# Two square-ReLU/leaky layers behind sparse attention: in-place sums, a moved group of products and full-row last values

## The chip, the cores and the metric

One core of one Trainium2 chip runs the whole program. The metric is device microseconds (us) from the first to the last instruction and what lies around them; lower is better. The kernel before takes 1148.19 us, the median of three runs (1145.18 to 1148.43).

## The reference

Attention over 4 batches of 8 heads, 576 positions, head width 64, in which scores more than `tau` below a row's maximum are dropped; then two layers of 512 to 2048 to 512 over the 2304 tokens. All is float32.

```python
scores = scale * np.matmul(q, k.transpose(0, 1, 3, 2))
thresh = np.max(scores, axis=-1, keepdims=True) - tau
scores = np.where(scores >= thresh, scores, -1000000000.0)
attn = softmax(scores)                      # written out in full in the reference
x = (attn @ v).transpose(0, 2, 1, 3).reshape(B * S, H * D)
h = x @ w_in;   x = (s * np.maximum(h, 0.0) ** 2 + b) @ w_out           # first layer
h = x @ w_in2;  g = np.maximum(h, 0.0) + alpha * np.minimum(h, 0.0)     # second layer
return g @ w_out2
```

## The kernel before, in words

**Who sets the order.** Nothing is scheduled while the chip runs. `add` records each step as a task with its engine, an assumed duration, the buffers that it reads and writes and a rank; a task may have two ways (DVE or POOL, say). `Plan.run` (L142) plays the tasks through once, when the program is built: whenever an engine is free, it takes the ready task of lowest rank whose buffers can be had. The order that comes out stands in each engine's queue, and an engine works its queue strictly in that order: an instruction that waits holds up all behind it. `SOON` is the lowest of the usual ranks, `LATER` a large one. A pool of buffers is a `Slots`; `caps` says how many of them a group may hold ("x": inputs of the second layer, "g": its hidden values).

**Stages, by the time in the trace.** Attention of batch 0 (pairs of heads 0 to 3) runs in plain fp32 up to about 145 us, the other batches in split form up to about 480 us, with the first part of layer 1 between them; the rest of layer 1 runs to 770 us (`blocks_b`, six blocks of 384 tokens); the first product of layer 2 to 958 us (three pairs of blocks); its second product to 1141.6 us (nine sub-blocks of 2 x 128 tokens).

**Split products.** Outside the plain attention, each product is three fp32r matmuls: `mm3` (L462) multiplies a low part by a high one, a high by a low, and a high by a high (L463, L464, L465). An operand's high part is an ACT copy to fp32r (L441), its low part the difference, on DVE or POOL (L442).

**Layer 2 by seven products.** Each product of 2 x 2 blocks is made of 7 products of sums of quarters instead of 8 (the Winograd form of Strassen's scheme). `seven` (L417) makes the operands: four sums of quarters (L433; t1 to t4 of inputs, s1 to s4 of hidden values), and for each of seven operands the high and the low part. They are used in the order `TURNS = (1, 2, 5, 6, 3, 7, 4)`; operands 1, 2 and 3 of the inputs are plain quarters, 5, 6, 7 and 4 are t1, t2, t3 and t4. t2 needs t1, and t4 needs t2. Each sum takes a new buffer of group "x" or "g". The quarters are loaded by the SP queue, and a pair's loads wait for the sums of the pair before (`xc`).

**First product of layer 2.** For each pair of blocks and each of eight groups of rows u, PE runs products 1, 2, 5, 6, 3 of this group and products 7 and 4 of the group before (`late7`, `late4`, L1122 and L1131), so that the DVE addition ahead of 7 and 4 (`plus`, L1114) has time. Behind it come the copies out of PSUM (`copy`, L1110) and `leaky` (L1075 to L1077: two ACT, one DVE), whose result goes to memory. The last group has no group behind it: its 7 and 4 follow directly (L1149). Layer 1's last block adds a part kept from earlier to each result (L1036) and stores it.

**Second product.** For each sub-block 4 turns l of 7 products from the hidden values; `copy` and `plus` (L1204) put the seven results together, `both` (L1208, DVE or POOL) adds two buffers, `store` (L1215) sends the rows out on the SP queue.

**Values of batch 0.** For a group of score tiles, `group` (L804) transposes five chunks of the weights (L818, L822), copies each to a buffer (gf or sh, L827) and multiplies it with the chunk's values (`product`, L831). The fifth chunk has only TL = 64 of 128 rows, and its product runs over these:

```python
nc.tensor.matmul(
    o.t[:, :n], lhsT=vt.t[:rows, c].rearrange("p h d -> p (h d)"), rhs=f.t[:rows, :n],
    start=c == 0, stop=c == NK - 1)
```

There are 16 such products (4 pairs, 4 groups each), 8 over 256 columns and 8 over 320. The trace shows each fp32 product as two matmuls.

## Time and profile before

| | |
|---|---|
| runs | 1148.19 us median, 1145.18 to 1148.43 |
| profiled execution | 1149.12 us, of which the span is 1147.1 us |
| PE busy | 1108.4 us, 97% of the span |
| DVE / ACT / POOL busy | 81% / 67% / 31% |
| chain that ended last | PE 66%, DVE 16%, ACT 9%, DMA 4% |
| issue of stores of the result | 56, all on the SP queue |

PE is the engine to watch: the chain of work that ended last is two thirds PE. A busy PE is not a PE at its peak, since the end of a matmul is modelled and matmuls overlap. What counts is the distance from one start to the next. In a stretch without waits it is 0.17 us for a split matmul of 384 columns and 0.12 us for one of 256. Times in a view are microseconds from the start of the span; "idle before" in brackets names what the engine waited for.

### The profile page before, as it was taken

How to read it: one execution, taken by the hardware profiler on the slowest of the kernel's cores; microseconds unless marked ns; L12 is line 12 of the kernel's file. 1: busy time of each engine (PE TensorE's matmuls, PEld its weight loads, DVE VectorE, ACT ScalarE, POOL GpSimd, SP SyncE). 2: the span in 40 equal slices, each digit the busy share in tenths (PEclk: the TensorE clock that was granted, in tenths of full speed). 3: DMA queues.
4: the chain of work that ended last, by engine and by line, in shares of the span. 5: the costliest groups of instructions: out<-in, count | busy, mean ns of one | idle time of the engine just before them, and what ended most of it. 6: DMA issues, size and time to landing. Idle time of an engine off the chain costs nothing.

```text
span 1147.1 us, 22073 instructions
## 1 busy us (share of the span) xinstructions
PE 1108.4 (97%) x7536; PEld 1052.3 (92%) x7536; DVE 934.2 (81%) x2040; ACT 764.2 (67%) x1744; POOL 358.7 (31%) x477
## 2 busy tenths in 40 slices
PE   8989999999999999999999999999999999999998
PEld 6667799999989999999999999999999998999998
DVE  5798887888978889847877788488975989899882
ACT  4787886877777878744444476366877987556551
POOL 2356663654664735500000012020211332112111
PEclk9999999999999999999999999998999999999999
DMA  5643354446435343134466564346724455455541
GB/s 120 162 141 122 102 142 110 110 100 156 101 88 129 100 109 93 37 109 155 123 218 210 182 214 157 124 133 206 261 103 162 138 189 161 116 143 153 139 116 37
DMA packets 183921, 156.92 MB, mean 137 GB/s; under 512 B 72192, under 2 KB 160768, under 8 KB 183808
## 3 DMA queue, kind: packets, MB, share of 16 engines
q1 hardware_dynamic: 183808, 155.51, 47.3%
q8 instruction: 59, 0.97, 0.4%
q14 instruction: 54, 0.44, 0.1%
HBM read 91.24 MB, written 44.56 MB: 118 GB/s over the span
## 4 chain that ended last, share of the span: by engine, by line
PE 66%; DVE 16%; ACT 9%; DMA 4%; issue 3%; SPq 1%; POOL 0%; POOLq 0%; DVEq 0%; ACTq 0%
PE bank L463 9%; PE bank L464 9%; PE bank L465 9%; PE bank_b L465 7%; PE bank_b L464 7%; PE bank_b L463 7%; PE sc L714 5%; PE bank L818 4%; PE bank L865 3%; DVE e L730 3%; DVE mx L724 2%; PE bank L831 2%; ACT e L728 2%; PE bank L822 1%; DVE wa L442 1%
## 5 line engine op out<-in xcount | busy, mean ns | idle before, releaser
L730 DVE SCALAR_TENSOR_TENSOR e<-sc,mx,e 128x576 f32<-128x576 f32 x144 | 116.6, 814 | 21.7 <-ACT e L728 18.5
L818 PE MATMUL bank<-eyes,e 128*128 128x128 f32 (+1 forms) x640 | 121.7, 277 | 1.7 <-DVE e L730 0.9
L728 ACT ACTIVATE e<-sc,mx 128x576 f32<-128x576 f32 x144 | 105.6, 737 | 26.4 <-DVE mx L724 25.4
L724 DVE TENSOR_REDUCE mx<-sc 128x1 f32<-128x576 f32 x144 | 107.4, 751 | 11.5 <-PE sc L714 10.2
L846 POOL TENSOR_TENSOR gl<-gf,gh 128x256 fp32r<-128x256 f32 (+1 forms) x96 | 78.0, 816 | 60.7 <-ACT gh L844 29.3
L818 PEld LDWEIGHTS bank<-eyes,e 128*128 128x128 f32 (+1 forms) x640 | 75.8, 134 | 21.9 <-issue 6.3
L463 PE MATMUL bank<-gt,wa 128*128 128x256 f32 (+1 forms) x271 | 84.9, 313 | 1.6 <-ACT rest L501 0.9
L463 PE MATMUL bank<-xt,wa 128*128 128x256 f32 (+1 forms) x266 | 82.8, 311 | 2.5 <-ACT rest L501 1.3
L464 PE MATMUL bank<-gt,wa 128*128 128x256 f32 (+1 forms) x271 | 81.2, 300 | 1.8 <-DVE gt L442 1.6
L465 PE MATMUL bank<-gt,wa 128*128 128x256 f32 (+1 forms) x271 | 80.7, 298 | 0.0
L465 PE MATMUL bank<-xt,wa 128*128 128x256 f32 (+1 forms) x266 | 76.8, 289 | 0.0
L464 PE MATMUL bank<-xt,wa 128*128 128x256 f32 (+1 forms) x266 | 76.7, 288 | 0.0
L726 POOL TENSOR_SCALAR mx<-mx,tau_s 128x1 f32<-128x1 f32 x144 | 46.7, 325 | 82.8 <-DVE mx L724 79.0
L714 PE MATMUL sc<-k,q 128*128 128x288 f32 x272 | 66.3, 369 | 3.4 <-DVE e L730 2.8
L865 PE MATMUL bank<-gl,vt 128*128 128x256 f32 (+1 forms) x192 | 64.4, 336 | 1.2 <-DVE gl L851 0.6
L464 PE MATMUL bank_b<-gt,wa 128*128 128x384 f32 (+1 forms) x169 | 55.3, 327 | 1.6 <-DVE gt L514 1.6
L865 PE MATMUL bank<-gh,vt 128*128 128x256 f32 (+1 forms) x192 | 56.5, 295 | 0.0
L521 ACT ACTIVATE rest<-bank 128x384 f32<-128x384 f32 x39 | 19.1, 490 | 55.6 <-PE bank L465 55.6
L463 PE MATMUL bank_b<-gt,wa 128*128 128x384 f32 (+1 forms) x169 | 55.4, 328 | 0.0
L714 PEld LDWEIGHTS sc<-k,q 128*128 128x128 f32 x272 | 44.2, 193 | 12.2 <-DVE e L730 5.1
L465 PE MATMUL bank_b<-gt,wa 128*128 128x384 f32 (+1 forms) x169 | 55.1, 326 | 0.0
L524 ACT ACTIVATE gt<-rest,b_b,s_b 128x384 fp32r<-128x384 f32 x56 | 39.4, 706 | 23.6 <-DVE rest L522 22.9
(654 smaller groups left out, 4170.5 us busy)
## 6 DMA issues: line engine op xcount, KB each, us to landing
stg<-in_moe_w_in_dram SPq DMA_DIRECT2D x32, 512.0 KB, 3.9
stg<-in_moe_w_out_dram SPq DMA_DIRECT2D x32, 512.0 KB, 3.8
qo<-hq SPq DMA_DIRECT2D x32, 256.0 KB, 4.3
rest<-gf SPq DMA_DIRECT2D x38, 128.0 KB, 3.0
ko<-hk SPq DMA_DIRECT2D x32, 144.0 KB, 2.5
xr<-xs SPq DMA_DIRECT2D x6, 768.0 KB, 4.9
yf<-yb SPq DMA_DIRECT2D x24, 192.0 KB, 3.1
gf<-rest SPq DMA_DIRECT2D x24, 192.0 KB, 1.9
```

The lines of the kernel that those rows point to most:

```text
L463: nc.tensor.matmul(o, lhsT=wl, rhs=mh, start=first, stop=False, skip_group_check=on_top)
L464: nc.tensor.matmul(o, lhsT=wh, rhs=ml, start=False, stop=False, skip_group_check=on_top)
L465: nc.tensor.matmul(o, lhsT=wh, rhs=mh, start=False, stop=last, skip_group_check=on_top)
L524: t = add("ACT", act(n, 2, True), lambda: nc.scalar.activation(g.t[:, 0, :n], r.t[:, :n], AF.Identity, bias=b_b, scale=s_b), (r,), (g,), r ...
L714: nc.tensor.matmul(sp.t[:, x, :HS], lhsT=o[0][:, c], rhs=o[1][:, x * HS:(x + 1) * HS], start=n == 0, stop=n == len(passes) - 1)
L724: add("DVE", dve(S), lambda sp=sp, mx=mx: nc.vector.tensor_reduce(mx.t[:, 0:1], sp.t[:, :, :HS], op=ALU.max, axis=AX.XY, negate=True), (sp ...
L726: t2 = add("POOL", 0.26, lambda mx=mx: nc.gpsimd.tensor_scalar(mx.t[:, 1:2], mx.t[:, 0:1], -1.0, tau_s, op0=ALU.mult, op1=ALU.subtract), ( ...
L728: add("ACT", act(S, 1), lambda sp=sp, mx=mx, e=e: nc.scalar.activation(halves(e.t), sp.t[:, :, :HS], AF.Exp, bias=mx.t[:, 0:1]), (sp, mx), ...
L730: add("DVE", dve(S) + 0.065, lambda sp=sp, mx=mx, e=e, col=col, sums=sums: nc.vector.scalar_tensor_tensor(halves(e.t), sp.t[:, :, :HS], mx ...
L818: nc.tensor.transpose(gt.t[:rows, m:m + P], es[i].t[:, c * P:c * P + rows], ident)
L846: add("POOL", pool2(n), lambda hi=hi, lo=lo, f=f: nc.gpsimd.tensor_tensor(lo.t[:, :n], f.t[:, :n], f32(hi.t[:, :n]), op=ALU.subtract), (f, ...
L865: nc.tensor.matmul(o.t[:, :n], lhsT=w, rhs=m.t[:, :n], start=c == 0 and x == 0, stop=c == NK - 1)
```

## The change

Five things change, in six places of the code.

1. In the first pair of the second layer, the sums take the place of quarters and sums that are no longer needed (t1 over quarter 11, t2 over t1, t3 over quarter 12, t4 over t2); a sum waits for those that read what it overwrites. In all pairs the sums of the inputs run on DVE alone. The caps of "x" and "g" go from 10 to 13 and from 8 to 12.
2. The additions of layer 1's last block get a later rank than before.
3. The last group's product 4 goes behind the first two products of the next stage, in front of its third.
4. `both` runs on DVE alone; a store may be issued by ACT where SP is busy, at rank LATER. As built, 24 of the 56 stores are on ACT.
5. The product of the fifth chunk runs over all 128 rows. The values behind row 64 are set to zero (4 memsets on POOL in place of 4 loads), and the gf and sh buffers are cleared once at the start (4 memsets).

```diff
-    t_s, sm_s = Slots(caps={"x": 10, "g": 8, "q": 6}), Slots()
+    t_s, sm_s = Slots(caps={"x": 13, "g": 12, "q": 6}), Slots()
...
-    def seven(quarters, left, n, tmp, group, to, to_group, rank, later=0.0):
-        have, sums, at = dict(quarters), [], 0.0
-        def ways(r):
-            return [("DVE", dve(n), r), ("POOL", pool2(n), r + later)]
+    def seven(quarters, left, n, tmp, group, to, to_group, rank, engines=("DVE", "POOL"), over={}):
+        have, sums, at, readers = dict(quarters), [], 0.0, {}
+        def ways(es):
+            return [(e, dve(n) if e == "DVE" else pool2(n), rank + at) for e in es]
...
-                b = Buf(tmp, group)
-                def a():
-                    return b.t[:, :n]
-                sums.append(add(ways(rank + at), 0, lambda e: on(e).tensor_tensor(a(), ax(), ay(), op=op), (bx, by), (b,), port=True))
+                if name in over:
+                    b, a = have[over[name]]
+                    after = readers.get(over[name], ())
+                else:
+                    b, after = Buf(tmp, group), ()
+                    def a():
+                        return b.t[:, :n]
+                t = add(ways(engines), 0, lambda e="DVE": on(e).tensor_tensor(a(), ax(), ay(), op=op), (bx, by), (b,), after=after, port=True)
...
+        for t in gf + sh:
+            nc.gpsimd.memset(t, 0.0)
...
+            if whole:
+                add("POOL", 0.2, lambda: nc.gpsimd.memset(nat["v"].t[TL:P, NQ], 0.0), (), (nat["v"],), rank=ready)
...
-                            o.t[:, :n], lhsT=vt.t[:rows, c].rearrange("p h d -> p (h d)"), rhs=f.t[:rows, :n],
+                            o.t[:, :n], lhsT=vt.t[:, c].rearrange("p h d -> p (h d)"), rhs=f.t[:, :n],
...
-                    (y, p), (t,), rank=SOON)
+                    (y, p), (t,), rank=SOON + 0.5 * (i == len(order) - 1))
...
-                ops, sums = seven(xq[c], False, n, t_s, "x", xb_s, None, SOON + 1e-3, LATER)
+                ops, sums = seven(xq[c], False, n, t_s, "x", xb_s, None, SOON + 1e-3, ("DVE",), {} if i else {"t1": "11", "t2": "t1", "t3": "12", "t4": "t2"})
...
-        for l in late7, late4:
-            for go in l:
-                go()
+        late7[0]()
...
-            t_s.caps["g"] += 8
-        add("POOL", 0.01, switch_d, after=(full[0],), rank=-2.0)
+            t_s.caps["g"] += 4
...
                     for k in TURNS:
+                        if late4 and k == TURNS[2]:
+                            late4.pop()()
+                            add("POOL", 0.01, switch_d, after=(full[0],), rank=-2.0)
...
-                    add([("DVE", dve(G1), rank), ("POOL", pool2(G1), rank)], 0, lambda e: on(e).tensor_tensor(
-                        x.t[:, :G1], x.t[:, :G1], y.t[:, :G1], op=ALU.add), (x, y), (x,), after=after, port=True)
+                    add("DVE", dve(G1), lambda: nc.vector.tensor_tensor(
+                        x.t[:, :G1], x.t[:, :G1], y.t[:, :G1], op=ALU.add), (x, y), (x,), after, rank, port=True)
...
-                        hwdge(lambda r0=r0, r=r, t0=t0, step=step: nc.sync.dma_start(
-                            out[t0:t0 + (r - 1) * step + 1:step, o:o + G1], x.t[r0:r0 + r, :G1]), (x,), (), SOON, 131)
+                        add([("SP", 0.6, SOON), ("ACT", 0.6, LATER)], 0, lambda e, r0=r0, r=r, t0=t0, step=step: (
+                            nc.sync if e == "SP" else nc.scalar).dma_start(
+                            out[t0:t0 + (r - 1) * step + 1:step, o:o + G1], x.t[r0:r0 + r, :G1]), (x,), (), tail=Plan.LAND + 0.7)
```

Since the order is made anew, it differs nearly everywhere in detail. Three places follow. The changed kernel's lines are shifted: L433, L442, L1036, L1077 and L1114 are L439, L452, L1053, L1094 and L1131 there, L463 to L465 are L474 to L476, L534 is L545 and L522 is L533.

DVE where layer 1 ends and layer 2 begins, before (L1036 adds a result of layer 1's last block from PSUM, L433 is a sum of quarters, the first two being both halves' t1):

```order
L534 TENSOR_TENSOR gt<-rest,gt 128x384
L1036 TENSOR_TENSOR yb_5759<-bank_b_5780,yat_5755 128x384
L1036 TENSOR_TENSOR yb_5757<-bank_b_5778,yat_5756 128x384
L433 TENSOR_TENSOR rest<-xr_5760,of_5765 128x384
L433 TENSOR_TENSOR rest<-xr_5760,of_5766 128x384
L1114 TENSOR_TENSOR rest<-bank_104,rest 128x384
L442 TENSOR_TENSOR xb_5773<-rest,xb_5773 128x384
L442 TENSOR_TENSOR gt<-rest,gt 128x384
L433 TENSOR_TENSOR rest<-xr_5760,rest 128x384
L1077 SCALAR_TENSOR_TENSOR rest<-rest,nal_b 128x384
L442 TENSOR_TENSOR gt<-rest,gt 128x384
```

The same place now:

```order
L533 TENSOR_TENSOR rest<-bank_b_5743,rest 128x384
L439 TENSOR_TENSOR of_5729<-xr_5723,of_5729 128x384
L439 TENSOR_TENSOR of_5728<-of_5730,of_5728 128x384
L452 TENSOR_TENSOR wb_5716<-sm_5726,wb_5716 128x256
L452 TENSOR_TENSOR wb_5716<-sm_5727,wb_5716 128x256
L545 TENSOR_TENSOR gt<-rest,gt 128x384
L452 TENSOR_TENSOR wb_5716<-sm_5724,wb_5716 128x256
L452 TENSOR_TENSOR wb_5716<-stg_98,wb_5716 128x256
L1131 TENSOR_TENSOR of_5730<-bank_106,of_5730 128x384
L366 TENSOR_SCALAR n_99<-n_99 128x512
L1053 TENSOR_TENSOR yb_5722<-bank_b_5742,yat_5718 128x384
L1053 TENSOR_TENSOR yb_5720<-bank_b_5741,yat_5719 128x384
```

Five sums (t1 and t3 of both halves, t2 of the first) stand further up still; the two here are t2 of the second half and t4 of the first, and L1053 comes behind them and behind L545, which ends the last squared hidden values of layer 1.

DVE where the second pair of blocks begins, before (L1077 ends `leaky`; the four L433 are t3 and t4 of both halves, the L442 behind them low parts of operands 7 and 4):

```order
L1077 SCALAR_TENSOR_TENSOR xr_5760<-xr_5760,nal_b 128x384
L1077 SCALAR_TENSOR_TENSOR of_5766<-of_5766,nal_b,yat_5755 128x384
L1077 SCALAR_TENSOR_TENSOR xr_5760<-xr_5760,nal_b,rest 128x384
L433 TENSOR_TENSOR yat_5756<-of_5767,rest 128x384
L433 TENSOR_TENSOR rest<-of_5768,xr_5760 128x384
L433 TENSOR_TENSOR n_100<-rest,yb_5757 128x384
L433 TENSOR_TENSOR yb_5758<-of_5765,yb_5759 128x384
L1114 TENSOR_TENSOR rest<-bank_b_5779,rest 128x384
L1077 SCALAR_TENSOR_TENSOR n_99<-n_99,nal_b,xr_5760 128x384
L442 TENSOR_TENSOR gt<-rest,gt 128x384
L442 TENSOR_TENSOR gt<-n_100,gt 128x384
L442 TENSOR_TENSOR gt<-yb_5758,gt 128x384
```

The second pair's sums now:

```order
L439 TENSOR_TENSOR rest<-n_100,xr_5723 128x384
L439 TENSOR_TENSOR xr_5723<-rest,of_5729 128x384
L439 TENSOR_TENSOR rest<-n_100,rest 128x384
L1094 SCALAR_TENSOR_TENSOR rest<-rest,nal_b 128x384
L439 TENSOR_TENSOR xr_5723<-rest,of_5731 128x384
L439 TENSOR_TENSOR rest<-yb_5721,rest 128x384
L1094 SCALAR_TENSOR_TENSOR yat_5719<-yat_5719,nal_b,of_5730 128x384
L1131 TENSOR_TENSOR yat_5718<-bank_104,yat_5718 128x384
L439 TENSOR_TENSOR rest<-yb_5722,xr_5723 128x384
L1131 TENSOR_TENSOR n_99<-bank_b_5740,n_99 128x384
L1094 SCALAR_TENSOR_TENSOR of_5731<-of_5731,nal_b,yat_5718 128x384
L452 TENSOR_TENSOR xt<-yb_5720,xt 128x384
```

All eight sums stand ahead of L452 on xt, the low part of the second half's operand 1; before, four of them stood behind the low parts of operands 2, 5 and 6 that DVE makes.

PE at the end of the first product of layer 2, before (128x384 is the second half of the last group's product 4, 128x256 the second product's first operand):

```order
L463 MATMUL bank_b2_5779<-gt_103,wb4_5753 128x384
L464 MATMUL bank_b2_5779<-gt_103,wb4_5753 128x384
L465 MATMUL bank_b2_5779<-gt_103,wb4_5753 128x384
L463 MATMUL bank1_105<-wb3_5752,wa9_96 128x256
L464 MATMUL bank1_105<-wb3_5752,wa9_96 128x256
L465 MATMUL bank1_105<-wb3_5752,wa9_96 128x256
```

The same place now:

```order
L474 MATMUL bank_b0_5740<-wa0_87,wa4_91 128x256
L475 MATMUL bank_b0_5740<-wa0_87,wa4_91 128x256
L476 MATMUL bank_b0_5740<-wa0_87,wa4_91 128x256
L474 MATMUL bank3_107<-gt_103,wb4_5716 128x384
L475 MATMUL bank3_107<-gt_103,wb4_5716 128x384
L476 MATMUL bank3_107<-gt_103,wb4_5716 128x384
```

Twelve matmuls of 128x256 (the second product's operands 1 and 2) stand ahead of the six of product 4; before, those six stood ahead of them and directly behind product 7.

## Rows read from the trace of the kernel before

**Rows 1.** Windows: per engine, busy us (count); last, PEclk, DMA share, GB/s.
```profile
18.00:145.00 127.00, 120.46 (x640) 89.04 (x639) 108.65 (x223) 100.45 (x221) 64.63 (x80) 1.00 0.49 132
145.00:505.00 360.00, 349.93 (x2767) 334.70 (x2765) 299.02 (x664) 271.24 (x613) 195.53 (x288) 1.00 0.42 105
770.00:780.00 10.00, 7.92 (x23) 6.00 (x23) 9.59 (x19) 6.85 (x15) 3.95 (x3) 0.66 0.56 207
800.00:825.00 25.00, 25.00 (x144) 24.76 (x143) 23.14 (x47) 19.63 (x48) 3.62 (x4) 1.00 0.89 291
963.50:1141.60 178.10, 178.10 (x1485) 177.91 (x1483) 146.70 (x406) 92.04 (x258) 28.83 (x31) 1.00 0.46 124
```

**Rows 2.** Timeline, PE, first attention stage: start us, us, what, [idle before <-releaser].
```profile
32.53 0.38 PE L818 MATMUL bank<-eyes,e 128*128 128x128 f32 x2
32.74 0.60 PE L831 MATMUL bank<-sh,v 128*128 128x256 f32 x2
33.18 0.38 PE L818 MATMUL bank<-eyes,e 128*64 128x128 f32 x2
...
35.23 0.38 PE L818 MATMUL bank<-eyes,e 128*128 128x128 f32 x2
35.54 0.70 PE L831 MATMUL bank<-gf,v 64*128 64x256 f32 x2
36.17 0.33 PE L818 MATMUL bank<-eyes,e 128*128 128x128 f32 x1
```

**Rows 3.** Timeline, PE, first layer to second.
```profile
770.01 0.34 PE L465 MATMUL bank_b<-gt,wb 128*128 128x384 f32 x1
...
780.21 0.33 PE L464 MATMUL bank_b<-xt,wa 128*128 128x384 f32 x1
```

**Rows 4.** Timeline, DVE, the same place.
```profile
768.82 1.08 DVE L1036 TENSOR_TENSOR yb<-bank_b,yat 128x384 f32<-128x384 f32 x2 [1.33 <-PE bank_b L465]
769.81 1.02 DVE L433 TENSOR_TENSOR rest<-xr,of 128x384 f32<-128x384 f32 x2
...
771.22 0.90 DVE L442 TENSOR_TENSOR xb<-rest,xb 128x384 fp32r<-128x384 f32 x1
772.03 1.37 DVE L442 TENSOR_TENSOR gt<-rest,gt 128x384 fp32r<-128x384 f32 x1
```

**Rows 5.** Waits, PE, 835 to 907 us: total us, times, longest.
```profile
PE bank_b L464 <- DVE xb L442: 1.4, 1, 1.4
PE bank L464 <- DVE gt L442: 1.1, 1, 1.1
PE bank L464 <- POOL xb L442: 0.5, 1, 0.5
```

**Rows 6.** Timeline, DVE, 838 to 843 us.
```profile
839.59 1.37 DVE L433 TENSOR_TENSOR yb<-of,yb 128x384 f32<-128x384 f32 x1
841.88 0.54 DVE L442 TENSOR_TENSOR gt<-rest,gt 128x384 fp32r<-128x384 f32 x1
```

**Rows 7.** Waits, PE, 950 to 963.5 us.
```profile
PE bank_b L463 <- DVE of L1114: 1.4, 1, 1.4
PE bank L463 <- DVE wb L442: 0.9, 1, 0.9
PE bank L463 <- DVE xt L442: 0.3, 1, 0.3
```

**Rows 8.** Timeline, PE, the longest of these waits.
```profile
955.41 0.34 PE L465 MATMUL bank_b<-xb,wb 128*128 128x384 f32 x1
...
957.43 0.34 PE L464 MATMUL bank_b<-gt,wb 128*128 128x384 f32 x1
```

**Rows 9.** Timeline, DVE, the end.
```profile
1142.98 0.43 DVE L1208 TENSOR_TENSOR of<-of,rest 128x256 f32<-128x256 f32 x1 [0.57 <-POOL xr L1208]
```

**Rows 10.** Timeline, SP queue, the end.
```profile
1142.97 1.11 SPq L1215 DMA_DIRECT2D out_dram<-xr  x2
1144.17 0.54 SPq L1215 DMA_DIRECT2D out_dram<-of  x1
```

16 lines of the change are left out of this document (11 added, 5 removed).

## Prediction

> **What bounds the kernel now.** I read the page first: PE is busy for 97% of the span and carries two thirds of the chain that ended last. So time can come back in two ways only: where PE works for longer than it must, or where it stands still. I therefore went along the starts of PE's matmuls and looked for distances above those of a stretch without waits (25 us by 144 matmuls, 0.1735 us each at 384 columns; 178.1 us by 1485, 0.12 us each at 256 [rows 1]), then asked the views of waits and timelines who was late there. The windows show where there is nothing to win: in the second product of layer 2 PE is busy for all of its 178.1 us [rows 1]. In the attention stages PE is idle for 127.00 - 120.46 = 6.5 us and 360.00 - 349.93 = 10.1 us [rows 1], spread over dozens of short waits. The rest of the standing still lies at the joints: layer 1 to layer 2, pair to pair, first product to second, and the end. The change touches each of these, and one place where PE works too long.
>
> **Full rows (part 5).** In plain attention, the two matmuls of a full product start 0.44 us before what follows (32.74 to 33.18), those of a 64-row product 0.63 us (35.54 to 36.17), and the two transposes ahead of it take 0.31 us from start to start instead of 0.21 (35.23 to 35.54 against 32.53 to 32.74) [rows 2]. So a 64-row product of 256 columns costs 0.19 us itself and 0.10 us ahead of it, 0.29 us in all. I take the 320-column ones to lose the same. Sixteen of them make 16 x 0.29 = 4.6 us of PE time, or 16 x 0.19 = 3.0 us if the distance ahead has another cause. PE is busy for 95% of that stretch [rows 1], so most of it reaches the end, but a part will turn into waiting for DVE (108.7 us busy of 127) [rows 1]: I take 3.6 us, from 2.0 to 4.6. The eight memsets are on POOL, half idle in that stretch [rows 1], and four loads fewer are on SP; both at nothing, covered by the loads with which the program starts, else some tenths of a us.
>
> Two rules of the Trainium skill bear on this. "TensorE: Matmul & The Clock Gate", section "LDWEIGHTS (loading the stationary operand)", says that the time of a weight load follows the columns and not the rows, so that 32 rows take as long as 128, and its table at the end says the same of a whole small matmul. By that the change saves nothing here, and the sum would be 3.6 us smaller. "TensorEngine Tiling (Array Packing)", section "Key Properties", says that a change of the tiling mode drains the engine. The rows agree with the second: the loss appears on entering the 64-row product, too.
>
> **Layer 1 to layer 2 (parts 1 and 2).** From 770.01 to 780.21 us PE starts 23 matmuls [rows 1, 3]; at 0.1735 us each they would take 4.0 us, so 6.2 us are lost. The cause is on DVE: two additions of layer 1's last block wait 1.33 us for PE, and the first sums t1 stand behind them, from 769.81 [rows 4]. PE wants t1's operand at 770.2. After that, the low parts of two halves follow each other slowly (0.90 and 1.37 us [rows 4], where 0.54 us is possible [rows 6]), and PE itself is slow: the granted clock of the window is 0.66 [rows 1], that is 1.2 GHz for two thirds of it and 2.4 for the rest. In the new order, t1, t2 and t3 stand far ahead of these additions, and operand 5 is made before PE gets there; so the first wait is gone. What is late next is product 3: DVE has, from the release of the first of these additions, eight instructions up to its first low part (two additions, two steps of a weight, operand 6's second low part, one `leaky`, t4, the low part itself), 8 x 0.55 = 4.4 us or a little more, while PE has three more results of layer 1 and products 5 and 6, 9 x 0.1735 + 12 x 0.1735 = 3.6 us. That leaves about 1 us, with the second half 1.5 us. The gain is 6.2 - 1.5 = 4.7 us. Its worst is 2.5 us: if the shorter wait still brings 1.2 GHz for a part of these 10 us (23 starts for 23 x 0.1735 = 4.0 us of work; 12 of them at half speed lose 2.1 us), or POOL's low part of operand 6, on which t4 waits, holds DVE up. Its best is 6.2 us.
>
> **Pair to pair (part 1).** PE waits 1.4, 1.1 and 0.5 us for low parts of operands 7 and 4 [rows 5]. At the first of the two joints the reason is plain: among the sums the last t4 takes 1.37 us from 839.59, and the low part of operand 7 comes only at 841.88 [rows 6]; at the second joint the same operand is late. A wait costs more than its idle time: from 955.41 to 957.43 are two steps from start to start, 0.35 us back to back, so 1.67 us are lost [rows 8] against 1.4 us idle [rows 7]. With 0.27 us more for each, these three waits are 3.0 + 0.8 = 3.8 us. With 13 buffers, the sums are all ahead of these low parts, and those of product 3, which stay on POOL, were in time before. I take 3.0 us back, from 1.5 to 3.8. The price is DVE time for two sums that POOL made, 2 x 0.55 us, in stretches where PE leads DVE by products.
>
> **First product to second (part 3).** Waits of 1.4, 0.9 and 0.3 us [rows 7], and 3 x 0.27 us, are 3.4 us. Product 4 waits for the addition behind product 7; twelve matmuls of 0.12 us, 1.4 us, are now between them, just what it waited. The second and the third wait are for the second product's sums (operands 5 on), which with 12 buffers of group "g" are made before the stage ends. I take 3.0 us, from 1.0 to 3.4. The lower end is for quarters that land late: ten more operands and sums are now queued in the last 20 us of the first product, on ACT and DVE ahead of its copies and additions, and where one waits for its load all behind it wait.
>
> **The end (part 4).** The last `both` starts at 1142.98, 0.57 us after DVE was free, since POOL's has to end first; SP then issues its store at 1144.17, behind two others from 1142.97 [rows 9, 10]. With both additions on DVE from 1142.4, at 0.43 us each, the last ends at about 1143.3 instead of 1143.4, and ACT issues its store right then instead of at 1144.17: 0.8 us, from 0.1 (only the addition) to 1.1. In the rest of the stage a store on ACT is hidden by idle time: ACT is busy for 92 of 178 us [rows 1], and 24 issues of 0.54 us [rows 10] are 13 us.
>
> **The sum.** 3.6 + 4.7 + 3.0 + 3.0 + 0.8 = 15.1 us. The order of attention and layer 1 is new in detail, too, without anything in it being aimed at; I put that at 0, from -3 to +3 us against 16.6 us of idle time there. Against the profiled execution, 1149.12 us, that is 1134.0 us; it is 0.9 us above the median of the runs, so the median would come to 1133.1. I say 1134, since what is left over tends to be a new wait that I do not see. The ends of the terms, as if independent, come together to some 4 us either way.
>
> **Rivals.** (a) Full rows bring nothing, because the distances are not due to the row count or another wait fills the freed PE time: 1134.0 + 3.6 = 1137.6 us. Rows 2 speak against it, the idle PE of that stretch for a little of it. (b) The joints keep half: DVE is the engine that is late at each of them, its work is only moved, and it stays the bound there. Then half of 10.7 us comes back, and 1134.0 + 5.4 = 1139.4 us; with 1.2 GHz once more, 1141. For it speaks DVE's load at a joint (9.59 of 10 us at the first [rows 1]); against it, that the moved sums had idle buffers as their only reason to be late. (c) The new order of the front part is worse: idle time there goes from 16.6 to 28 us, and 1134 + 11 = 1145 us, within the measurement's reach of no change. Nothing in the views speaks for it but the length of that part. (d) Slower: stores on ACT. ACT works its queue in order, so a store that waits for DVE's addition holds up the high parts of the operands behind it. If the operands' lead over PE in the second product were below that wait, each of 24 stores would cost its issue and the addition, 0.54 + 0.42 us, or 23 us: 1134 + 23 = 1157 us. It decides from a lead under 1 us; against it stands a PE that is busy without a gap for 178 us [rows 1], which tells of a long lead.
>
> **How the numbers follow.** My case 0.62 (1129 to 1139), (a) 0.10, (b) 0.16, (c) 0.07, (d) 0.05. A measurement of this kernel can tell about 0.3%, 3.4 us. Below 1144.7 us lie my case, (a) and (b): faster 0.88; (c) is the same, 0.07; (d) slower, 0.05. The range has to leave out no more than 0.2: from 1128, all gains at their best but one, to 1144, past (b).
>
> **What would show it.** In the changed profile: 64-row forms of the product are gone, and each last chunk of 256 columns starts 0.44 us before what follows; less than 2.5 us lost between layer 1's last matmul and the second group of layer 2, with the granted clock at 2.4 GHz there; no wait for operand 7 at the joints of pairs; product 4 without a wait for L1131; `both` twice on DVE and the last store on ACT. Wrong would be a PE that waits in the second product, an idle time above 20 us up to 505 us, or 1.2 GHz at the first joint.

## The result

The changed kernel takes 1129.33 us, the median of five runs (1127.45 to 1130.36), against 1148.08 us of the kernel before in the same comparison (1145.18 to 1148.43): a ratio of 0.984 with a 95% interval of 0.9825 to 0.9855, 18.8 us less. The profiled execution took 1129.05 us, with a span of 1127.3 us, 19.8 us less than the span before.

The views in the order in which the prediction asked for them follow, all of the changed kernel; lines are shifted as told at the diff, and L831 is L848 there, L818 is L835, L1204 is L1221, L1208 is L1225 and L1215 is L1233. First the windows, to be held against [rows 1] (columns as there):

```profile
18.00:145.00 127.00, 119.86 (x679) 94.99 (x678) 111.93 (x228) 103.68 (x229) 69.03 (x83) 1.00 0.50 133
145.00:505.00 360.00, 352.19 (x2785) 336.70 (x2784) 309.26 (x694) 270.55 (x611) 181.82 (x272) 1.00 0.44 109
514.00:517.50 3.50, 3.50 (x19) 3.50 (x19) 2.80 (x5) 0.76 (x2) 0.00 (x0) 0.51 0.61 156
760.00:780.00 20.00, 19.33 (x110) 18.74 (x110) 19.34 (x41) 14.60 (x33) 0.00 (x0) 1.00 0.71 231
940.00:1122.10 182.10, 182.09 (x1513) 181.69 (x1511) 151.05 (x413) 95.95 (x270) 29.21 (x34) 1.00 0.45 124
```

In the second product of layer 2 PE is busy without a gap, as before. The stretch where layer 1 ends now runs at 2.4 GHz (1.00, where [rows 1] had 0.66), and PE is busy for 19.33 of 20 us. Up to 505 us PE is idle for 7.1 + 7.8 = 15.0 us, where [rows 1] has 16.6. The third row is new here: at 514 us, where layer 1's first part ends and its second begins, the clock is at 1.2 GHz for 3.4 us. The kernel before had such a stretch there, too (520.6 to 524.0 us); the change didn't aim at it.

The fifth chunk's products are now among those of 128 rows. All eight of 256 columns start 0.43 to 0.44 us before what follows; one of them:

```profile
53.28 0.59 PE L848 MATMUL bank<-gf,v 128*128 128x256 f32 x2
53.72 0.60 PE L835 MATMUL bank<-eyes,e 128*128 128x128 f32 x4
```

All that is left of PE's waits from 527 us to its end, in 595 us (engine, line, waited for: total us, times, longest):

```profile
PE bank L475 <- DVE gt L545: 1.1, 2, 0.9
PE bank L475 <- DVE gt L452: 0.7, 1, 0.7
PE bank_b L474 <- ACT of L1127: 0.6, 2, 0.3
PE bank_b L474 <- ACT rest L1127: 0.3, 1, 0.3
```

The waits of [rows 5] and [rows 7] are all gone. The longest at a joint is 0.7 us for a low part (L452) where layer 2 begins. PE and DVE there (timeline: start us, us, what, idle before):

```profile
766.13 0.34 PE L474 MATMUL bank<-gt,wa 128*128 128x384 f32 x1
767.14 0.44 PE L475 MATMUL bank<-gt,wa 128*128 128x384 f32 x1 [0.67 <-DVE gt L452]
767.42 0.34 PE L476 MATMUL bank<-gt,wa 128*128 128x384 f32 x1
```

```profile
762.81 1.02 DVE L1053 TENSOR_TENSOR yb<-bank_b,yat 128x384 f32<-128x384 f32 x2
...
765.07 0.55 DVE L452 TENSOR_TENSOR gt<-of,gt 128x384 fp32r<-128x384 f32 x1
765.53 0.61 DVE L1094 SCALAR_TENSOR_TENSOR rest<-rest,nal_b,of 128x384 f32<-128x384 f32 x1
766.06 0.55 DVE L439 TENSOR_TENSOR of<-of,of 128x384 f32<-128x384 f32 x1
766.53 1.02 DVE L452 TENSOR_TENSOR gt<-xr,gt 128x384 fp32r<-128x384 f32 x2
```

It is the first low part of product 3, as the prediction had it, behind the eight instructions that it counted: from the additions of layer 1 at 762.81 over two steps of a weight (the rows left out), a low part, a `leaky` and t4 to the low part that ends at 767.08, 4.3 us where it had 4.4. PE waits 0.67 us for it.

At the end of the first product PE goes from product 7 (938.69) to two products of 256 columns, then to product 4 at 940.81, and on, without a wait that the trace marks:

```profile
939.03 0.33 PE L476 MATMUL bank<-gt,wb 128*128 128x384 f32 x1
939.21 0.28 PE L474 MATMUL bank_b<-wb,wa 128*128 128x256 f32 x1
...
940.51 0.28 PE L476 MATMUL bank_b<-wa,wa 128*128 128x256 f32 x1
940.81 0.45 PE L474 MATMUL bank<-gt,wb 128*128 128x384 f32 x1
```

The last store is issued by ACT at 1123.83, 1.72 us behind the end of PE (1122.11); before, it was 2.55 us behind it (1144.17 and 1141.62):

```profile
1122.82 0.41 DVE L1225 TENSOR_TENSOR yb<-yb,rest 128x256 f32<-128x256 f32 x1
1123.27 0.42 DVE L1225 TENSOR_TENSOR rest<-rest 128x256 f32<-128x256 f32 x1
```

```profile
1123.26 0.47 ACTq L1233 DMA_DIRECT2D out_dram<-yb  x1
1123.83 0.54 ACTq L1233 DMA_DIRECT2D out_dram<-rest  x1
```

To compare kernels by stage, I count for each joint the time lost: from the first start of a matmul to the last in that stretch, less the number of steps times 0.1735 us (384 columns) or 0.12 us (256). "Front" is the start of the first matmul of 384 columns, that is, attention and the first part of layer 1. "First joint" is layer 1 to layer 2, "pairs" all of the first product behind it, "C to D" the joint of the two products with the first sums behind it. The column on 1.2 GHz is for the first joint alone. The table is worked out from the traces, one execution of each kernel, of all runs but the last two; what the runs are is told below.

| run | time, us | front | first joint lost | 1.2 GHz there | pairs lost | C to D lost |
|---|---|---|---|---|---|---|
| before | 1148.1 | 533.3 | 6.2 | 6.8 us | 7.2 | 3.6 |
| changed | 1129.3 | 526.7 | 1.2 | 0 | 2.4 | 0.3 |
| part 5 alone (e1_rows) | 1140.3 | 528.2 | 6.4 | 6.8 us | 4.8 | 3.6 |
| part 1 alone (e2_sums) | 1137.8 | 533.8 | 1.2 | 0 | 2.7 | 1.6 |
| part 2 alone (e3_rank) | 1144.8 | 531.1 | 3.2 | 0 | 6.5 | 3.5 |
| part 3 alone (e4_late) | 1148.8 | 533.6 | 5.6 | 3.4 us | 5.8 | 4.4 |
| all but part 5 (e6_no_rows) | 1135.1 | 531.3 | 1.2 | 0 | 4.1 | 0.3 |
| changed, 96 rows (e7_96) | 1128.9 | 529.1 | 1.2 | 0 | 1.8 | 0.3 |
| all but part 3 (e9_no_late) | 1130.2 | 526.0 | 1.2 | 0 | 1.6 | 1.6 |
| all but part 2 (e10_no_rank) | 1130.0 | 528.2 | 1.7 | 0 | 1.0 | 0.1 |
| caps alone (f1_caps) | 1142.0 | 530.7 | 6.4 | 6.8 us | 2.7 | 1.5 |
| in place, DVE alone (f2_inplace) | 1142.7 | 532.7 | 1.2 | 0 | 4.9 | 3.6 |

Two columns carry noise that one must know. The front differs between executions of one order: the five kernels with 128 or 96 rows show the same order of PE's matmuls there and come to 526.0 to 529.1 us, the seven with 64 rows show one other order and come to 530.7 to 533.8 us. A part of the spread is the clock: up to the end of the front it is at 1.2 GHz not at all, for 3.4 or for 6.8 us, depending on the execution. Since the rows and the order go together in these twelve, the column alone can't tell one from the other. And the pairs differ by some us with any new order: 1.0 to 2.4 us in the four runs that have parts 1 and 5, 4.8 to 7.2 in those where nothing of the pairs' code was touched.

### The profile page after: what moved, and what is told of

Read it like the earlier page. It is cut to its first block, busy times and chain, and to the rows that moved or that the text cites. A ratio compares the mean times of both kernels' runs of the same rounds, so it can differ in the third digit from the quotient of the medians.

```text
span 1127.3 us, 22120 instructions
## 1 busy us (share of the span) xinstructions
PE 1098.4 (97%) x7536; PEld 1051.0 (93%) x7536; DVE 932.4 (83%) x2051; ACT 763.5 (68%) x1744; POOL 348.2 (31%) x474
## 4 chain that ended last, share of the span: by engine, by line
PE 65%; DVE 18%; ACT 7%; DMA 3%; issue 3%; POOL 2%; SPq 1%; DVEq 0%; ACTq 0%; POOLq 0%
PE bank L474 9%; PE bank L475 9%; PE bank L476 9%; PE bank_b L474 7%; PE bank_b L475 7%; PE bank_b L476 7%; PE sc L731 4%; PE bank L835 4%; PE bank L882 3%; DVE e L747 3%; DVE mx L741 2%; ACT e L745 2%; DMA stg<-in_moe_w_in_dram 1%; DVE wa L452 1%; DVE n L368 1%
## 5 line engine op out<-in xcount | busy, mean ns | idle before, releaser
L835 PE MATMUL bank<-eyes,e 128*128 128x128 f32 (+1 forms) x640 | 119.9, 276 | 5.8 <-DVE gr L875 1.4
L745 ACT ACTIVATE e<-sc,mx 128x576 f32<-128x576 f32 x144 | 105.7, 738 | 19.7 <-DVE mx L741 18.8
L835 PEld LDWEIGHTS bank<-eyes,e 128*128 128x128 f32 (+1 forms) x640 | 76.3, 134 | 23.5 <-DVE gr L875 2.6
L474 PE MATMUL bank<-xt,wa 128*128 128x256 f32 (+1 forms) x262 | 81.4, 311 | 1.1 <-ACT rest L512 1.0
L474 PE MATMUL bank<-gt,wa 128*128 128x256 f32 (+1 forms) x258 | 79.6, 309 | 1.1 <-ACT rest L957 0.7
L475 PE MATMUL bank<-gt,wa 128*128 128x256 f32 (+1 forms) x258 | 76.0, 294 | 0.9 <-DVE gt L452 0.7
L476 PE MATMUL bank<-xt,wa 128*128 128x256 f32 (+1 forms) x262 | 75.8, 289 | 0.0
L476 PE MATMUL bank<-gt,wa 128*128 128x256 f32 (+1 forms) x258 | 75.8, 294 | 0.0
L475 PE MATMUL bank<-xt,wa 128*128 128x256 f32 (+1 forms) x262 | 75.7, 289 | 0.0
L474 PE MATMUL bank_b<-gt,wa 128*128 128x384 f32 (+1 forms) x177 | 58.2, 329 | 1.0 <-ACT gt L524 0.7
L475 PE MATMUL bank_b<-gt,wa 128*128 128x384 f32 (+1 forms) x177 | 58.1, 328 | 1.0 <-DVE gt L525 1.0
L476 PE MATMUL bank_b<-gt,wa 128*128 128x384 f32 (+1 forms) x177 | 57.8, 326 | 0.0
L474 PEld LDWEIGHTS bank<-xt,wa 128*128 128x128 f32 x262 | 49.7, 190 | 2.8 <-ACT rest L512 2.3
```

Of the source, the lines that this page charges most:

```text
L474: nc.tensor.matmul(o, lhsT=wl, rhs=mh, start=first, stop=False, skip_group_check=on_top)
L475: nc.tensor.matmul(o, lhsT=wh, rhs=ml, start=False, stop=False, skip_group_check=on_top)
L476: nc.tensor.matmul(o, lhsT=wh, rhs=mh, start=False, stop=last, skip_group_check=on_top)
L745: add("ACT", act(S, 1), lambda sp=sp, mx=mx, e=e: nc.scalar.activation(halves(e.t), sp.t[:, :, :HS], AF.Exp, bias=mx.t[:, 0:1]), (sp, mx), ...
L835: nc.tensor.transpose(gt.t[:rows, m:m + P], es[i].t[:, c * P:c * P + rows], ident)
```

## The experiments

Each edit is made anew into an order for all engines, so that no run differs from its neighbour in one place only; the table above says where it differs in time. Parts have the numbers of the list of the change.

**One part at a time, on the kernel before.** Part 5 alone, the full rows:

```diff
-                            o.t[:, :n], lhsT=vt.t[:rows, c].rearrange("p h d -> p (h d)"), rhs=f.t[:rows, :n],
+                            o.t[:, :n], lhsT=vt.t[:, c].rearrange("p h d -> p (h d)"), rhs=f.t[:, :n],
```

with the memsets and without the four loads.

> The kernel before with part 5 alone (fifth chunk's product over 128 rows, memsets in place of four loads). Theory A, the row count costs: sixteen products lose 0.29 us each, 4.6 us of PE time, of which 3.6 reach the end: 1144.5 us against 1148.1, 0.9969. In the profile the fifth chunk's product starts 0.44 us before what follows (256 columns), the transposes ahead take 0.21. Rival N, rows don't matter: the distances stay 0.63 and 0.31 us and the time 1148. Rival M, the new order of the front part is what counts: the time lies anywhere within 3 us of 1148, with the distances gone all the same. In all of them the joints behind 505 us keep their waits: about 6 us lost at layer 1 to layer 2, about 4 at the pairs, about 4 at first to second product.

Measured: 1140.29 us, ratio 0.9923 (0.9902 to 0.9944). The front is 5.1 us shorter. Another 2.4 us came back at the pairs, which this part doesn't touch: in the new order the waits at one of the two joints of pairs are gone. So the time alone would say too much for the rows; the stage says 5.1 us, of which the noise of the front is a part, and the front's order is new as well. Rival M, the new order, is thus not excluded by this run's time; that the rows cost 0.29 us each is read from the distances, below.

Part 1 alone, sums in place, on DVE, and caps:

```diff
-    t_s, sm_s = Slots(caps={"x": 10, "g": 8, "q": 6}), Slots()
+    t_s, sm_s = Slots(caps={"x": 13, "g": 12, "q": 6}), Slots()
...
-                ops, sums = seven(xq[c], False, n, t_s, "x", xb_s, None, SOON + 1e-3, LATER)
+                ops, sums = seven(xq[c], False, n, t_s, "x", xb_s, None, SOON + 1e-3, ("DVE",), {} if i else {"t1": "11", "t2": "t1", "t3": "12", "t4": "t2"})
```

> The kernel before with part 1 alone (sums in place in the first pair, sums on DVE alone, caps 13 and 12); the additions of layer 1's last block keep their rank, product 4 its place. Theory A, the sums had no buffer: they were late since the pool had none for them until layer 1 had ended, so sums in place are enough; the 6.2 us of the first joint shrink to 1.5 or less, the pairs give back 3, the second and third wait of first to second product (1.2 + 0.5 us) too; the wait of product 4 for its addition, 1.4 us, stays: 1148.1 - 4.7 - 3.0 - 1.5 = 1139 us. Rival B, the additions' rank is what counts: two additions that wait for PE still stand ahead of the sums or the low parts, the first joint keeps over 4 us and 1.2 GHz: 1148.1 - 1.5 - 3.0 - 1.5 = 1142 us. Rival C, caps don't matter at the pairs because DVE is the bound: waits for operand 7 stay, 1144 us or more.

Measured: 1137.75 us, ratio 0.9903 (0.9886 to 0.992). All of PE's waits from the first joint on:

```profile
PE bank_b L474 <- DVE yat L1125: 1.3, 1, 1.3
PE bank_b L474 <- ACT xr L1121: 0.9, 2, 0.7
PE bank L475 <- DVE gt L452: 0.7, 1, 0.7
PE bank_b L474 <- ACT yb L1121: 0.5, 1, 0.5
```

The first joint is as good as in the whole change, without the later rank (the 0.7 us for L452), no operand is late at a pair, and what is left is the wait of 1.3 us for the addition (L1125) ahead of product 4. That is theory A; B and C fall. This part holds one step more than the list of the change says: the low parts of these inputs, where POOL makes them, now have the ordinary rank and no longer LATER. In the traces POOL makes 14 of these 42 low parts here and 13 in the changed kernel, against 12 before.

Part 2 alone, the rank of the additions:

```diff
-                    (y, p), (t,), rank=SOON)
+                    (y, p), (t,), rank=SOON + 0.5 * (i == len(order) - 1))
```

> The kernel before with part 2 alone (a later rank for the additions of layer 1's last block). Theory A, the sums had no buffer: without buffers the sums come when they came, the first joint keeps 4 to 6 us of its 6.2, 1146 to 1148 us. Rival B, the rank is what counts: with the additions behind the sums the first joint shrinks to 1.5 us lost and 2.4 GHz throughout, 1143.4 us. All else unchanged, so the other joints lose what they lost.

Measured: 1144.82 us, ratio 0.9968 (0.9955 to 0.9982). It is between both: 3.2 us are lost at the first joint instead of 6.2, and the clock stays at 2.4 GHz there. The rank alone is worth something, since the sums no longer stand behind additions that wait; but the whole change without it (below) loses only 0.5 us more there.

Part 3 alone, product 4 behind two products of the next stage:

```diff
-        for l in late7, late4:
-            for go in l:
-                go()
+        late7[0]()
...
                     for k in TURNS:
+                        if late4 and k == TURNS[2]:
+                            late4.pop()()
```

> The kernel before with part 3 alone (the last group's product 4 behind two products of the second product; caps as before). Theory A: the wait of 1.4 us for the addition goes, 1.7 us with the restart; the waits of 0.9 and 0.3 us for the second product's operands stay or grow to about 1.5 in all, since the hidden values' sums still lack buffers and PE comes to these operands 1.4 us earlier: 1146.4 to 1147.8 us. Rival D, the wait only moves: all that product 4 gave back is lost at the next operand, 1148 us.

Measured: 1148.75 us, ratio 1.001 (0.9993 to 1.0026), no change. PE's longest waits behind 900 us:

```profile
PE bank L463 <- DVE wb L442: 2.3, 1, 2.3
PE bank_b L464 <- DVE xb L442: 1.4, 1, 1.4
```

and the window behind the first of them (columns as in [rows 1]):

```profile
960.00:963.20 3.20, 3.20 (x18) 3.20 (x17) 3.20 (x11) 2.12 (x6) 0.00 (x0) 0.50 0.81 224
```

The wait for the addition is gone, and a wait of 2.3 us for the second product's low part (L442 on wb) has taken its place, where the kernel before had 1.4 + 0.9 + 0.3 us [rows 7]. Behind it TensorE runs at 1.2 GHz for 3.4 us (granted clock 0.50), which the three shorter waits had not brought; so 4.4 us are lost at C to D instead of 3.6. About 1.7 us of the 4.4 are due to that clock in this one execution (half of 3.4 us); without them, by this estimate, the part would have gained 0.9 us there. Most of the wait moved, as rival D has it: 2.3 of 2.6 us are left. Without the cap of group "g" the next operands' low parts are no earlier.

**What it is in part 1.** The caps alone, and the sums in place and on DVE with the old caps:

```diff
-    t_s, sm_s = Slots(caps={"x": 10, "g": 8, "q": 6}), Slots()
+    t_s, sm_s = Slots(caps={"x": 13, "g": 12, "q": 6}), Slots()
```

> The kernel before with the caps alone (x 13, g 12 and 4 more later); sums still take new buffers in every pair and may run on POOL. Theory A: the caps cure the pairs and the second product's operands (3 + 1.5 us), the sums in place cure the first joint, where the pool's buffers, not the cap, are short until layer 1 has ended: the first joint keeps 5 to 6 of its 6.2 us and 1.2 GHz; 1148.1 - 4.5 = 1143.6 us. Rival E, the cap holds the sums up at the first joint, too: it shrinks to under 2 us there, 1139 us.

```diff
-                ops, sums = seven(xq[c], False, n, t_s, "x", xb_s, None, SOON + 1e-3, LATER)
+                ops, sums = seven(xq[c], False, n, t_s, "x", xb_s, None, SOON + 1e-3, ("DVE",), {} if i else {"t1": "11", "t2": "t1", "t3": "12", "t4": "t2"})
```

> The kernel before with the sums in place in the first pair and on DVE alone, caps as before (10 and 8). Theory A: the first joint shrinks to about 0.8 us lost (0.84 with all of part 1); the pairs and the second product's operands keep about 4 and 1.5 us: 1148.1 - 5.4 = 1142.7 us. Rival E, the cap holds the sums up at the first joint: nothing changes there, 1148 us.

Measured: 1142.01 us, ratio 0.9946 (0.9924 to 0.9967), and 1142.69 us, ratio 0.9953 (0.9939 to 0.9967). Each cures its own places. Where DVE makes the sums t1 of the first pair, with caps alone (L433) and in place (L439):

```profile
766.17 1.08 DVE L1036 TENSOR_TENSOR yb<-bank_b,yat 128x384 f32<-128x384 f32 x2 [1.35 <-PE bank_b L465]
767.16 1.02 DVE L433 TENSOR_TENSOR rest<-xr,of 128x384 f32<-128x384 f32 x2
```

```profile
743.45 1.02 DVE L439 TENSOR_TENSOR of<-xr,of 128x384 f32<-128x384 f32 x2
```

With 13 in the cap, t1 still comes at 767.16, behind additions that wait 1.35 us for PE, since the pool has no free buffer until layer 1 has ended: it writes `rest`, a buffer that the kernel gives to the pool only behind layer 1's last products. In place it writes `of`, comes 24 us earlier, and the first joint loses 1.2 instead of 6.4 us. The second kernel also keeps the sums off POOL and changes the rank of low parts on POOL, and no run takes these from the sums in place; but with the caps alone t1 was on DVE, too, so being on DVE does not make it early. For the pairs and the second product it is the other way round: the caps leave 2.7 of 7.2 us at the pairs and 1.5 at C to D (the addition ahead of product 4 again), in place leaves 4.9 and keeps all 3.6. Rival E falls twice.

**The whole change less one part.** Without part 5 (its lines as before, 64 rows), and with 96 rows instead of 128:

```diff
-                            o.t[:, :n], lhsT=vt.t[:, c].rearrange("p h d -> p (h d)"), rhs=f.t[:, :n],
+                            o.t[:, :n], lhsT=vt.t[:P if c < NQ else 96, c].rearrange("p h d -> p (h d)"), rhs=f.t[:P if c < NQ else 96, :n],
```

> The changed kernel without part 5 (64-row products and the four loads are back). Theory A, row count: 16 products x 0.29 us and what the front gained in the run with part 5 alone (5.1 us): the front up to the first product of 384 columns takes 4.6 to 5.5 us longer, 1134 to 1135 us against 1129.3, all joints of the second layer as in the changed kernel. Rival M, the gain of the front was the new order of that build: less than 2 us longer, 1129 to 1131.

> The changed kernel with the fifth chunk's product over 96 rows instead of 128 (the 32 rows left out hold zeros). Theory A1, the loss belongs to the smaller tile into which 64 rows put TensorE: the trace shows 96 rows as a tile of 128 rows, the product starts 0.44 us before what follows, the transposes ahead 0.21, and the time is that of the changed kernel, 1129.3. Theory A2, the loss belongs to rows that are left out, whatever their number: 96 rows lose part of 0.29 us, 0.1 us or more each, 1131 us or more. Rival N (rows don't matter) has the same distances as A1, but then has to explain the 64-row distances otherwise.

Measured: 1135.06 us, ratio 0.9887 (0.9865 to 0.9909), and 1128.91 us, ratio 0.983 (0.9802 to 0.9859). Without full rows the profiled span is 6.2 us longer: 4.6 us in the front, and 1.7 us at the pairs, where this order has one wait of 1.6 us. Without full rows the front also has the old order of PE's matmuls again, so rival M is not excluded by this time either. PE in the run with 96 rows, around one of these products:

```profile
53.35 0.60 PE L835 MATMUL bank<-eyes,e 128*64 128x128 f32 x4
53.79 1.14 PE L731 MATMUL sc<-k,q 128*128 128x288 f32 x4
54.76 0.60 PE L848 MATMUL bank<-gf,v 96*128 96x256 f32 x2
55.20 0.60 PE L835 MATMUL bank<-eyes,e 128*128 128x128 f32 x4
```

96 rows start 0.44 us before what follows (54.76 to 55.20), just as 128 do, where 64 rows take 0.63 [rows 2]; all eight of 256 columns are alike in this. So what costs is not the number of rows that are left out (A2 falls). And the distances answer rival M: with 64 rows each of the products has the longer one, in the traces of before and e6_no_rows alike (320 columns: 0.73 against 0.54 us), so that sixteen come to 16 x 0.29 = 4.6 us, about what the fronts differ by.

The trace shows where the time goes. Weight loads (PEld) in the kernel before, of a full product, of a 64-row product and of the transposes behind it:

```profile
32.64 0.30 PEld L831 LDWEIGHTS bank<-sh,v 128*128 128x128 f32 x2
35.54 0.29 PEld L831 LDWEIGHTS bank<-gf,v 64*128 64x128 f32 x2 [0.17 <-issue]
36.17 0.20 PEld L818 LDWEIGHTS bank<-eyes,e 128*128 128x128 f32 x2 [0.33 <-issue]
```

The full product's first load starts 0.10 us ahead of its matmul (32.64 and 32.74 [rows 2]), under the matmul before it. The 64-row product's starts with its matmul (35.54 both), and so does the load behind the product (36.17 both). It is so in all sixteen, while with 96 rows the first loads mostly start 0.11 or 0.24 us ahead. So the 64 rows lose the overlap of loading and multiplying where PE enters the product and where it leaves it.

What I wrote of the form in the trace was wrong: it shows 96*128, the shape of the weights, and no tile. That 64 rows put TensorE into another tile, and 96 don't, fits all of this, but no run shows it directly. The Trainium skill, "TensorEngine Tiling (Array Packing)", section "Tiling Modes", lists 64x128 as a tile of its own and none of 96 rows, which agrees.

Without part 3, and without part 2 (the lines shown above as before, the caps as changed):

> The changed kernel without part 3 (product 4 of the last group directly behind product 7). By the run with part 1 alone, where 1.5 us were lost on the addition ahead of product 4 and nothing behind it: 1.5 us more, 1130.8 us, one wait of 1.3 to 1.4 us before product 4. If part 3 is worth what the prediction gave it (3.0 us): 1132.3 us, with waits at the second product's operands as well.

> The changed kernel without part 2 (the additions of layer 1's last block at their old rank). Theory A, buffers were the cause of the first joint: nothing changes there beyond some tenths of a us, since part 1 alone left 0.84 us lost of 6.2 and the whole change leaves 0.83: 1129.3 us, within 1 us. Rival B, the rank is needed: over 2 us lost at the first joint, 1131.5 us or more.

Measured: 1130.21 us, ratio 0.9846 (0.9824 to 0.9869), and 1130.01 us, ratio 0.9841 (0.9816 to 0.9866). Neither can be told from the whole change by its time. By the stages one can: C to D loses 1.6 us without part 3, on the wait for its addition alone,

```profile
PE bank L474 <- DVE of L1131: 1.3, 1, 1.3
```

so in the whole change part 3 is worth 1.3 us. Without part 2 the table has 1.7 instead of 1.2 us at the first joint, but the joint itself is the same. PE's waits there, and behind it up to 900 us:

```profile
PE bank L475 <- DVE gt L452: 0.7, 1, 0.7
PE bank_b L474 <- ACT of L1127: 0.2, 1, 0.2
```

The first is the wait of the whole change, 0.67 us in both. The second, 0.5 us with its restart, is for a copy out of PSUM on ACT, 7.6 us later; the rank has no part in it. So theory A holds, and no run shows a worth of part 2 once the sums have buffers.

**A better version.** The largest of PE's losses that is left behind attention lies at 510 to 517 us: waits of 0.7, 0.7 and 0.2 us for the last squares of layer 1's first part, and 3.4 us at 1.2 GHz. Two kernels let products of the second part go there. The first allows any of them, as soon as the products for the second half of the last block's results have begun:

```diff
-        full = [last]
+        full = list(full)
```

> The changed kernel, in which the first products of layer 1's second part (384 columns) may go among the last products of its first part, one word in the order: PE's waits at that joint were filled with nothing (1.8 us lost on two waits and 1.2 GHz for 3.5 us, where TensorE does half, 1.7 us). If the waits bring the lower clock there, both go: 3.5 us less, 1125.8 us, with 2.4 GHz throughout from 500 to 530 us. If the lower clock there has nothing to do with these waits, it stays: 1.8 us less, 1127.5 us. If the squares of the first part come later by the new products ahead of them, the wait moves: 1129 us.

Measured: 1136.44 us, ratio 0.9906 (0.9882 to 0.993), 7 us slower than the changed kernel. PE's waits there, and the windows:

```profile
PE bank_b L474 <- ACT gt L535: 2.8, 1, 2.8
PE bank_b L475 <- DVE gt L545: 1.4, 1, 1.4
PE bank_b L475 <- DVE gt L525: 1.0, 2, 0.7
PE bank_b L474 <- ACT gt L524: 0.7, 1, 0.7
```

```profile
500.00:530.00 30.00, 28.35 (x217) 27.75 (x216) 26.76 (x49) 12.41 (x22) 0.00 (x0) 1.00 0.48 152
540.00:550.00 10.00, 7.65 (x27) 7.39 (x28) 10.00 (x22) 7.34 (x13) 1.01 (x1) 0.66 0.34 106
```

The old waits (L525, L524) are still there: the new products were allowed only behind them. They are then used up, and PE waits 2.8 and 1.4 us for the first squares of the second part, and 1.2 GHz comes there (0.66 from 540 to 550) instead of at 514. All three expectations missed; the last came nearest.

The second allows one hidden product only, and from the last hidden product of the first part on:

```diff
+            of_h = last
...
-        full = [last]
+        full, fence = [of_h], [(), (last,)]
...
-                h, full[0] = hidden(x, n, (f,), u1i, seq[0], (full[0],))
+                h, full[0] = hidden(x, n, (f,), u1i, seq[0], (full[0], *fence[0]))
+                fence[:] = fence[-1:]
```

> The changed kernel, in which one hidden product of layer 1's second part (four steps of three matmuls, 2.1 us) may go among the last products of its first part; all others come behind that part, as before. It stands, in the new order, between the products that waited. If PE's waits there (1.8 us lost) bring the lower clock behind them (1.7 us lost), both go and the time is 3.5 us less, 1125.8 us, with 2.4 GHz from 500 to 530 us. If the new product only moves the waits (the squares' chain on ACT and DVE is as long as before, and what PE did behind it is missing there): 1129 us, with a wait of 1 to 2 us some us later, and the lower clock behind that.

Measured: 1126.43 us, median of five (1124.12 to 1127.40), ratio 0.9811 (0.9791 to 0.9831). It is the fastest kernel of this case, 2.9 us below the changed one by the medians; since the two were not run together, and their intervals against the kernel before overlap a little, the size is not sure. The windows (columns as in [rows 1]) for the changed kernel, for this one and, for comparison, for the changed kernel without part 2 (e10_no_rank), whose code at this place is the changed kernel's:

```profile
500.00:530.00 30.00, 28.35 (x211) 27.74 (x210) 25.44 (x46) 12.61 (x22) 0.00 (x0) 0.94 0.52 154
```

```profile
500.00:530.00 30.00, 29.93 (x235) 29.72 (x234) 26.66 (x48) 13.13 (x23) 0.00 (x0) 1.00 0.53 163
```

```profile
500.00:530.00 30.00, 28.36 (x228) 27.76 (x227) 27.13 (x50) 13.78 (x25) 0.00 (x0) 1.00 0.47 151
```

PE is busy for 29.93 instead of 28.35 us: the waits are gone, 2.4 us by the distances of the starts (the 1.8 us that were expected leave out the third wait and one restart). The clock is at 1.00 instead of 0.94, but that is not shown to come of it. The kernel without part 2 has the same waits at this place and stays at 2.4 GHz there, as f3_fill does, so the clock differs from one execution to the next; and the mean granted clock of the five executions is 0.998 for the changed kernel and for this one alike. So the waits explain 2.4 of the 2.9 us between the medians, and the 1.7 us for the clock are seen in one execution only.

## Why the prediction was right, point by point

The forecast was 1134.0 us, from 1128 to 1144; measured were 1129.3. Each place that the prediction named gave time back, by the step that it named, and the gain came out larger: 18.8 us instead of 14 or 15. By the terms of its sum, with the profiled executions:

| term | predicted | measured | from |
|---|---|---|---|
| full rows | 3.6 | 4.7 | fronts of the table: mean 527.6 of the five with full or 96 rows, 532.4 of the seven with 64 |
| first joint | 4.7 | 5.0 | 6.2 to 1.2 |
| pairs | 3.0 | 4.8 | 7.2 to 2.4 |
| C to D | 3.0 | 3.3 | 3.6 to 0.3 |
| the end | 0.8 | 0.4 | from PE's end to the span's: 5.5 to 5.15 |
| sum | 15.1 | 18.2 | |

The rest up to the 19.8 us between the spans is, to 0.3 us, the front of this execution, 526.7, which lies below its mean of 527.6, and that of before, 533.3, which lies above.

**Full rows** were right in price (0.29 us, 16 times, 4.6 us) and mis-sized in what reaches the end. I took 1 us off, because DVE is busy for 108.7 of 127 us in that stretch [rows 1] and PE would wait for it more. DVE's load rose to 111.9 us, but PE did not wait more: its idle time up to the end of the front is 22.0 us in the mean of the five traces and 22.3 in that of the seven. So the discount has no ground in the traces. The two means of the fronts alone would not decide it, since by their spread the 4.7 us is uncertain by some 1.7 us (an estimate, 95%), and they carry the new order as well; the 0.29 us are from the distances. The rival by which the row count brings nothing fell with the distances of e6_no_rows and e7_96. Where it went wrong is not the load: 64 rows of weights load in 0.184 us and 128 in 0.190 (means in the kernel before). The Trainium skill, "TensorE: Matmul & The Clock Gate", section "LDWEIGHTS (loading the stationary operand)", says that the time of a load does not follow the rows; the trace agrees. What the rival left out is that these loads no longer start ahead.

**The first joint** was right in its step: the sums' place on DVE was the cause, product 3 is late next, and it loses 0.8 us where I had 1 to 1.5. What I had not separated is why the sums were late. I named both the additions ahead of them and the buffers; f2_inplace, e2_sums and e10_no_rank show that free buffers are enough, and that the later rank then adds nothing; without them it took 3.0 of the 6.2 us (e3_rank).

**Pairs** were the term most off. The three waits of [rows 5] are all gone, 3.8 us with their restarts, the most that the prediction gave them; it took 3.0. The other 1.0 us is mostly waits for copies out of PSUM on ACT (L1110 before: 0.4, 0.6 and 0.8 us), which the prediction left out and the change doesn't aim at; in the new order they are 0.3 us each. That is luck. The runs with nothing but another part of the change show how little that is a property of the edit: 4.8 to 7.2 us are lost at the pairs there.

**C to D** was right in its sum, and the run with part 3 alone shows that it needs the caps: without them the 1.4 us that product 4 gave back are waited at the next operand, and in that execution the lower clock came on top. The prediction gave the second and third waits to the 12 buffers, and that holds (f1_caps). Its fear, quarters that land late, didn't come true.

**The end** was right in its mechanism and too large. The last store is issued 0.83 us earlier after PE's end, as forecast, but the span ends only 0.36 us earlier: the last landing took 2.3 us instead of 2.1, and what lies behind it is 0.3 us longer. In the other traces this stretch is 4.9 to 5.2 us with part 4 and 5.5 to 5.7 without. No run has part 4 alone, so its two halves, `both` on DVE and stores on ACT, aren't told apart.

**Rivals.** That the joints keep half because DVE is the bound there fell: DVE is busy for 19.34 of 20 us at the first joint, and PE loses 1.2 us. DVE had the work to do in any case; what it lacked were buffers to do it early (f2_inplace for the first joint, f1_caps for the pairs). That stores on ACT slow the second product fell too: PE is busy for 182.09 of 182.10 us there. A worse front did not come; a front that differs by up to 3 us between executions of one order did, and that is the grain in which this kernel's edits have to be read.

## What to carry to other kernels

When an engine is busy nearly all of the time at a joint and the next one waits for it, ask first what keeps its work from being done earlier: here it was free buffers, by two different limits (the pool's at one place, a group's cap at another), and not the engine. A step moved past a wait gives nothing as long as the step behind it is late by as much, so a moved product and the buffers for the operands behind it belong together. And where an edit makes a new order for everything, read the stage that it aims at and not the total: the rest moves by a few us of its own accord. Even a stage can mislead, where every kernel with the edit has one order and every kernel without it another, as the front here; there the distances between single instructions decide. And one execution's clock is no property of the kernel until a second one shows it.

## What the runs showed of the hardware

A matmul of fp32 over 64 rows of weights takes 0.31 us for 256 columns from start to start, and the transposes ahead of it 0.09 to 0.10 us longer; over 96 or 128 rows it takes 0.22 us and nothing ahead. The load of its weights is no longer (0.184 us against 0.190), but where PE goes from 128 rows to 64 and back, the load starts with its matmul (0.00 us ahead, in all sixteen products of the kernel before), where else it mostly runs under the matmul before. Transposes whose weights have 64 columns (128*64 in the trace, four of them from 53.35 to 53.79 us in e7_96, 0.11 us each) show no such loss. The Trainium skill, "TensorEngine Tiling (Array Packing)", section "Key Properties", has a drain at every change of the tiling mode; the distances fit that for 64 rows and show no drain for weights of 64 columns. Which mode either of them sets the trace doesn't show.

The clock did not follow one length of a wait, nor the same waits each time. In the changed kernel three waits of 0.7, 0.7 and 0.2 us (L524 and L525, up to 513.7 us) were followed by 1.2 GHz from 514.1 us for 3.4 us; the same three waits in e10_no_rank and f3_fill were not. With the first joint losing 3.2 us in e3_rank the clock stayed at 2.4 GHz, where the joints that lost 6.2 to 6.4 us (before, e1_rows, f1_caps) went with 6.8 us of 1.2 GHz. And three waits of 1.4, 0.9 and 0.3 us [rows 7] left the clock alone in the kernel before (1.00 from 950 to 964 us), while one of 2.3 us in their place was followed by 3.4 us of 1.2 GHz in the one trace of e4_late. Whether waits gathered into one cost more than the same time in pieces, one trace of each doesn't tell.
